# Another hand-written sequence of tasks for a kernel of local attention and an S4 convolution

## The chip, the core and the metric

The kernel runs on one core of a Trainium2 chip. The metric is the device time of one execution, in microseconds. The core has five engines with a queue each, and each queue is worked off in order: TensorE (PE in the profile; its weight loads are shown as PEld), VectorE (DVE), ScalarE (ACT), GpSimd (POOL) and SyncE (SP). In this kernel SP and POOL do little but start transfers (DMA).

## The reference

Two branches see the same input x (2048 positions, 640 channels) and are mixed by a gate.

```
g = sigmoid((x * gate_w).sum(-1))
# A: 32 heads of 20, each position attends to 8 positions, 2 apart, behind it
qkv = x @ wqkv ; logits = q . k[pos - 2*w] * 20**-0.5, w = 0..7 ; a = (softmax(logits) . v) @ wo
# B: a state space filter of 192 states for each channel, as a convolution over 2048 positions
K[d, l] = Re sum_n C[d,n] * exp(dt*A[d,n]*l) * dt*B[d,n]
y = irfft(rfft(pad(x)) * rfft(pad(K)))[:2048] + x * Dskip
return g * a + (1 - g) * y
```

## The kernel before

The work is written as tasks. `Plan.add` puts a task on a list with its possible engines, the tasks it depends on, and the ring of buffers that it takes or gives back. A task issues a few instructions of one engine, or the transfers of one step. Nothing is scheduled at run time: `Plan.order` reads a string of `ORDER` (steps from one task number to the next, with a letter where a task with a choice takes the engine that isn't its first one), and `Plan.emit` issues the tasks in that sequence, each engine keeping its own part of it in order. So the string fixes the order in each of the five queues and, for evictions from PSUM, whether ACT or DVE does them. There are two strings: "main" with 1274 tasks and "tail" with 304.

The names that matter below, in the order in which data flows:

- The front. `turn`, `tev` (L204, L507): PE transposes x in ten pieces, each evicted. `late`, `lev` (L311): 60 pieces of the qkv projection, five matmuls each, in two halves (`late5`, `late5b`), each evicted by `lev`; the first ten are q and k of the first 512 positions. On ACT and DVE the parameters of the filter are made (`SSMParams`: L624 to L661) and stored in ten planes by SP (`sp0` to `sp9`, Sprm). `gate`, `gexp`, `gsig`, `gturn`, `gtwice` (L219 to L239) make the gate.
- The filter generator (`KGen`), ten rounds c = 0 to 9. `L` (L766) loads the planes, `arg` (L801, PE) makes 15 pieces of arguments a round into a ring of two PSUM buffers (`ar`), `act` (L816 Sin, L818 Exp, ACT) evaluates them, `pq` (L838, L840, DVE) multiplies them, three instructions for each of three units, and `kmm` (L856, PE) contracts them: 4 quarters for each unit, of 16 matmuls (32 for the middle unit) in tiles of 128x32 or 64x32. `fin` evicts a round. After rounds 4 and 9 the half of the filter is spread through DRAM (`own`, `other`, `xst`, `xld`: Kx, kc).
- The attention, eight chunks. `prod` (L375, DVE, five a chunk) and `lg` (L381, PE) make logits; `max`, `neg`, `exp`, `sum`, `at` the softmax; `ast` and `asb` take it through DRAM (SP), `vc` loads v (POOL, L368, from vS that `lst` stores); `pv` (L449, DVE) weighs, `gat` (L456, PE) sums, `oT` evicts, `wo` (L480, PE) projects, `ga` evicts with the gate (L489 on ACT, L491 on DVE), `gaS` stores.
- The first transforms: `f1`, `fu`, `fk` (L1300, L1319, PE) of filter and input, with evictions `f1e`, `fue`, `fke` of 1024 columns (halves for some fk). `rows` (L1003, L1004, POOL) loads the input for them in eight steps, each waiting for the one before.
- The tail (`fft_conv`): second transforms `fp` with evictions `sp` in eight blocks, complex products `ta`, `tc`, `Y` on DVE, inverse transforms `inv` with evictions `cp`, then `yp`, evicted and mixed with the attention branch (`tt`, `mx`, `st`), and `out`. SP loads `tphi3` to `tphi7` (PHI, PHX), `paced0` to `paced6` (psi, then gaF).

PE works with different forms of tiles: 128x128 (projections, transforms), 64x128 (arg), 128x32 (logits, kmm), 64x32 (kmm of the middle unit), 128x64 (gat).

## Time and profile before

| | |
|---|---|
| runs | 337.15, 334.77, 336.39 us; median 336.39 |
| span of the profiled execution | 335.4 us (no other time of that execution is shown) |
| first Sin of the generator on ACT | 55.2 us |
| first product of the generator on DVE | 65.5 us |
| end of the main plan, first transform of the tail | 266.5 us |
| last eviction of the output | 328 us |

The page gives busy times of the engines and their share of the span, groups of instructions by source line with the mean duration of one and the idle time ahead of them, and waits by what ended them. A line like L507 or L509 is that of a helper (`evict`), so its groups are told apart by their tiles. A matmul's end is modelled, so what PE waits for is read better from its weight loads (PEld). "issue" is waiting in which no other engine is seen to be the cause.

### The profile page before, as it was taken

Reading aid. Unit: us, or ns where it says so; the run is one execution under the profiler, and the core shown is the slowest. Engines: PE = TensorE matmul, PEld = TensorE weight load, DVE = VectorE, ACT = ScalarE, POOL = GpSimd, SP = SyncE. Lnnn points to the kernel's source line nnn. Section 1 sums busy time; section 2 is a strip of 40 time slices with the busy share of each in tenths; the row PEclk is TensorE's granted clock in tenths of the full one; section 3 lists DMA queues with packets and bytes.
Section 4 is the critical chain, followed back from the end, with each engine's and each line's share of the span. In section 5 each row is a group of like instructions: output and inputs, shape, how many; then the busy total and the mean of one; then the engine's idle time right before and its main releaser. Section 6 shows DMA issues by size and latency. Waiting matters only on the chain. (4 is left out here: it accounts for less than half of the span.)

```text
span 335.4 us, 11982 instructions
## 1 busy us (share of the span) xinstructions
PE 285.5 (85%) x5181; PEld 171.0 (51%) x5214; DVE 294.2 (88%) x401; ACT 293.4 (87%) x433; POOL 62.3 (19%) x94
## 2 busy tenths in 40 slices
PE   0367999997899999999998799999999899996850
PEld 0334563444445555445554344556677676665740
DVE  1997988798989999999999979999686799999881
ACT  1789736999899999999999799999987889998990
POOL 8700043020005000101412341211040000000062
PEclk9999999999999999999999989999999999999985
DMA  8984435437107110524874887365565527666056
GB/s 253 356 264 113 119 91 159 86 91 170 26 9 153 27 24 8 149 62 141 199 190 119 186 208 161 93 118 124 154 207 221 180 64 216 159 123 100 4 136 182
DMA packets 45975, 45.68 MB, mean 136 GB/s; under 512 B 25098, under 2 KB 39738, under 8 KB 45922
## 3 DMA queue, kind: packets, MB, share of 16 engines
q1 hardware_dynamic: 39928, 27.90, 30.3%
q0 software_dynamic: 5248, 16.39, 20.2%
q8 instruction: 41, 0.67, 0.9%
q10 hardware_dynamic: 746, 0.61, 0.6%
q14 instruction: 12, 0.10, 0.1%
HBM read 30.88 MB, written 14.01 MB: 134 GB/s over the span
## 5 line engine op out<-in xcount | busy, mean ns | idle before, releaser
L311 PE MATMUL tb<-bufA 128*128 128x512 bf16 x267 | 73.5, 391 | 4.2 <-issue 1.4
L816 ACT ACTIVATE big<-ar 128x740 bf16<-128x740 int16 (+1 forms) x72 | 56.7, 858 | 1.4 <-PE ar L801 1.2
L818 ACT ACTIVATE big<-ar 128x848 bf16<-128x848 f32 x60 | 50.1, 905 | 0.2
L801 PE MATMUL ar<-Rarg,L 64*128 64x212 bf16 (+4 forms) x600 | 46.5, 253 | 3.5 <-ACT big L816 1.9
L449 DVE TENSOR_TENSOR pv<-vc,asb 128x2048 bf16<-128x2048 bf16 x40 | 48.2, 1217 | 0.3 <-PE tb L456 0.3
L311 PEld LDWEIGHTS <-bufA 128*128 128x128 bf16 x300 | 31.2, 122 | 28.5 <-issue 12.3
L856 PEld LDWEIGHTS <-pt 128*32 128x32 bf16 (+1 forms) x2560 | 25.3, 92 | 35.7 <-issue 33.2
L856 PE MATMUL kps<-qq,pt 128*32 128x21 bf16 (+1 forms) x2560 | 36.6, 173 | 6.0 <-issue 5.1
L838 DVE TENSOR_TENSOR pt<-big 128x1024 bf16<-128x1024 bf16 x48 | 32.8, 701 | 4.3 <-ACT big L816 2.2
L801 PEld LDWEIGHTS <-L 64*128 64x128 bf16 x600 | 20.8, 94 | 25.2 <-issue 22.4
L480 PE MATMUL tb<-wo_sb,oT 128*128 128x320 bf16 x160 | 29.9, 306 | 0.2
L507 ACT ACTIVATE sp_u<-fp 128x640 bf16<-128x640 f32 x31 | 23.9, 953 | 0.8 <-PE fp L1073 0.8
L375 DVE TENSOR_TENSOR prod<-prj 128x2048 bf16<-128x2048 bf16 x20 | 24.0, 1218 | 0.2 <-PE lg L381 0.2
L375 DVE TENSOR_TENSOR prod<-qA,kA 128x2048 bf16<-128x2048 bf16 x20 | 23.9, 1217 | 0.2 <-PE lg L381 0.2
L507 ACT ACTIVATE sp_k<-fp 128x640 bf16<-128x640 f32 x29 | 22.6, 969 | 1.1 <-PE fp L1073 1.1
L456 PE MATMUL tb<-pv,ind 128*64 128x512 bf16 (+1 forms) x192 | 23.2, 353 | 0.0
L368 POOL DMA_DIRECT2D vc<-vS x16 | 11.5, 723 | 59.0 <-DVE pv L449 55.0
L840 DVE TENSOR_TENSOR qq<-big 128x1344 bf16<-128x1344 bf16 x24 | 21.2, 883 | 0.0
L1191 POOL DMA_DIRECT2D out_dram<-ot x14 | 7.7, 558 | 72.3 <-DVE ot L1173 72.3
L1073 PEld LDWEIGHTS <-PHI 128*128 128x128 bf16 x160 | 15.5, 97 | 8.1 <-issue 1.1
L489 ACT ACTIVATE ga<-tb,g_sb 128x320 bf16<-128x320 f32 x29 | 15.6, 550 | 3.4 <-PE tb L480 3.1
L480 PEld LDWEIGHTS <-oT 128*128 128x128 bf16 x160 | 13.1, 98 | 7.1 <-issue 3.1
(171 smaller groups left out, 547.9 us busy)
## 6 DMA issues: line engine op xcount, KB each, us to landing
vc<-vS POOLq DMA_DIRECT2D x16, 327.5 KB, 6.4
xn<-in_A_x_dram SPq DMA_DIRECT2D x4, 640.0 KB
gaS<-ga SPq DMA_DIRECT2D x8, 320.0 KB
Usb<-in_A_x_dram POOLq DMA_DIRECT2D x8, 320.0 KB, 5.7
gaF<-gaS SPq DMA_DIRECT2D x8, 320.0 KB
bufA<-in_A_wqkv_dram SPq DMA_DIRECT2D x3, 800.0 KB
Sprm<-pc SPq DMA_DIRECT2D x10, 240.0 KB
L<-Sprm SPq DMA_DIRECT2D x76, 30.0 KB
```

The costliest lines, as they stand in the source:

```text
L311: nc.tensor.matmul(ppf, self.wq[:, which, kt, e::5], self.xT[:, c0 // 1024, kt, c0 % 1024:c0 % 1024 + SC], start=(kt == 0), stop=(kt == NK ...
L375: nc.vector.tensor_tensor(b[e][:], q[:, e, o:o + C].unsqueeze(1).to_broadcast([128, W, C]), win(k[:, e, :], o, W, DIL, C), ALU.mult)
L449: nc.vector.tensor_tensor(o, vw, b["asb"][:].unsqueeze(2).to_broadcast(sh), ALU.mult)
L456: nc.tensor.matmul(b["op", e][64 * a:64 * a + 64, 0:n, :], ind[:, 32:96], b["pv", e][:, w, a, 0:n, :], start=(w == 0), stop=(w == 3), skip ...
L480: nc.tensor.matmul(apf[:, :320], b["oT"][:, e, i * 128:(i + 1) * 128], wo_sb[:, e, hf * 320:(hf + 1) * 320], start=(e == 0), stop=(e == 4))
L507: nc.scalar.activation(o, i, ACT.Identity)
L801: nc.tensor.matmul(ar[:, g2, a0:a0 + ncol], L[rows, sb, gv, l0:l0 + 128], R[rows, c0:c0 + ncol], start=True, stop=True, tile_position=(64 ...
L816: nc.scalar.activation(d_[:, :, s0 * QW:s1 * QW], ar[:].bitcast(I16)[:, :, 0:2 * (s1 - s0) * QW:2], ACT.Sin, scale=SCL)
L818: nc.scalar.activation(dst[:, gp::2].rearrange("p g s n -> p g (s n)"), ar[:, :, 0:2 * EW], ACT.Exp)
L838: nc.vector.tensor_tensor(pt[:, :, k, :], gg[:, :, ::-1] if k else gg, e1, ALU.mult)
L840: nc.vector.tensor_tensor(qq[:], trg[:, :, KI:].rearrange("p a (v m) -> p a v m", v=2), exq[:, :, KI:].unsqueeze(2).to_broadcast([128, 32, ...
L856: nc.tensor.matmul(kps[32 * g:32 * g + 32, h, NM * ql:NM * ql + NM], pt[rows, k, v, :], qq[rows, k, v, :], start=(g not in started), stop= ...
```

## The change

Only the two strings of `ORDER` change. No task is added or dropped, no instruction differs in form; the sequence does, and for 22 + 22 tasks of "main" and 6 + 7 of "tail" the choice of engine (DVE to ACT, and ACT to DVE).

```diff
 ORDER = {"main": (
-    "7 -7 15 -14 1 1166 -1164 56 -57 3 2 -3 6 1 1 39 -43 1 51A -8A -25 -14 2 38 1D 1 1A -32 33 1A -42 1 69 1 -57 72 -56 57 "
...
+    "7 53 -45 -15 1 3 1 6 -8 -1 4 6 -4 53 -48 -4 1 13 29 1 -29 -10 2 38 1D 1 1 1 1 28 1 1080 -1140 -11 1 4 11D 1 55 -58 1 "
...
 ), "tail": (
-    "3 1A 7 1A -7 1D 1 6 1A -6D 1 1A 10 -5 1A 1 1A 3 13 1D -13 1 1 2 1A 3 1A -3 1A -4 11 1A 6 -11 1A 11 -6 1A 1 1A -41 1 "
...
+    "5 -2 1D 2 5 -4 5D 1 1D 6 -12 1 1 11 13 1 -20 2 -1 2D 20 -2 3 -2 -11 1 -5 1 1 1 3 1 14 -13 2 -1 2 11 -4 1 4 1 1 1 -48 1 "
...
```

Written out by name, the parts of the queues that are spoken of below:

```
DVE, front
- mk5 stt_at near_t1 near_t0 mk7 mk6 tev7 tev5 tev8 lev9 prod00 prod01 gsig lev18 prod02 lev35
+ mk5 lin_t1 stt_t1 stt_at stt_at near_t1 near_t0 mk6 mk7 prod00 prod01 prod02 gsig prod03 lev35
PE, front
- turn7 late3b late8 late8b late6 turn5 late6b turn8 late15 late9 late15b late9b gate late11 late18 late11b late18b
-   lg00 lg01 late35 late25 gturn late35b late25b lg02 late28 late27 arg00000
+ late4 late4b turn6 late9 late9b late7 late7b late1 late1b late15 late15b late11 late11b gate
+   lg00 lg01 late18 late18b late35 late35b gturn lg02 arg00000
PE, a piece of round 3 to 4
- arg40000 kmm222 lg32 lg33 kmm223 arg40001 late40b late43 kmm300 arg40010 arg40100 late43b late45 kmm301 lg34
+ arg30200 late40 late40b arg30201 kmm300 kmm301 kmm302 kmm303 arg30210 lg32 late43 arg40000 arg40001
SP, main
- L0S L1 ast0 L2 asb0 L3 ast1 ... xst1S gaS6 xld1S gaS7
+ L0S L1 ast0 asb0 L2 L3 ast1 ... xst1S gaS6 xld1S gaS7
POOL, main
- consts L0G lst02 vc0 vc256 lst12 wo vc512 dskip lst22 lst32 gst rows0 vc768 rows1 xst0G rows2 vc1024 rows3 rows4
-   xld0G rows5 vc1280 rows6 vc1536 rows7 gates0 vc1792 xst1G xld1G phi0 gates1 phi1 gates2 phi2 gates3
+ consts wo dskip L0G gst lst02 vc0 vc256 lst12 vc512 lst22 vc768 lst32 rows0 rows1 rows2 rows3 xst0G vc1024 xld0G
+   vc1280 rows4 rows5 rows6 rows7 phi0 gates3 gates0 gates1 gates2 phi1 vc1536 vc1792 phi2 xst1G xld1G
SP, tail
- tphi3 tphi4 tphi5 paced0 paced1 tphi6 tphi7 paced2 paced3 paced4 paced5 paced6
+ tphi3 tphi4 tphi5 tphi6 paced0 paced1 paced2 paced3 paced4 tphi7 paced5 paced6
```

On DVE the evictions tev5, tev7, tev8, lev0, lev9, lev14 and lev18 leave for ACT, and mk4, mk8 and lin_t1 come from it. On PE the quarters of kmm, which stood mostly one by one between other tasks, stand in groups of two to six; between neighbouring PE tasks of "main" the form of the tiles changes 380 times in the old sequence and 280 times in the new one.

## The prediction

> **What bounds the kernel now.** The page is read first for whether one engine carries the span, then the busy time by stage, then what each engine waited for.

> ```profile
> span 335.4 us, 11982 instructions
> PE 285.5 (85%) x5181; PEld 171.0 (51%) x5214; DVE 294.2 (88%) x401; ACT 293.4 (87%) x433; POOL 62.3 (19%) x94
> ...
> 65.50:100.00 34.50, 31.05 (x696) 16.11 (x703) 30.55 (x43) 32.24 (x46) 1.93 (x3) 1.00 0.31 72
> 100.00:186.00 86.00, 82.02 (x1885) 43.37 (x1901) 83.50 (x117) 85.85 (x131) 15.68 (x25) 1.00 0.44 108
> 186.00:198.00 12.00, 9.64 (x191) 4.14 (x187) 9.50 (x11) 9.45 (x16) 4.44 (x4) 0.86 0.82 208
> 198.00:235.00 37.00, 35.61 (x989) 20.95 (x986) 36.40 (x46) 36.09 (x53) 8.58 (x13) 1.00 0.59 128
> 235.00:266.50 31.50, 29.41 (x247) 22.31 (x244) 24.81 (x37) 28.09 (x42) 4.37 (x8) 1.00 0.58 197
> ...
> 65.50:266.50 201.00, 187.72 (x3992) 106.88 (x4013) 184.75 (x250) 191.71 (x283) 34.99 (x52) 0.99 0.49 125
> 55.20:266.50 211.30, 197.28 (x4067) 111.15 (x4095) 192.72 (x262) 201.98 (x296) 36.90 (x55) 0.99 0.50 126
> ```

> The columns of a stretch are its length and the busy time of PE, PEld, DVE, ACT and POOL, then the granted clock. No engine carries the span alone. From 55.2 us, where ScalarE's first Sin runs, to 266.5, where the main plan ends, ACT is busy 201.98 of 211.30 (9.3 idle). From 65.5, where the first product of the filter generator runs, DVE is busy 184.75 of 201.00. Its 16.3 us of idle time are 4.0 before 100, 2.5 to 186, 2.5 around 190, 0.6 to 235 and 6.7 at the end. So a new order wins by starting this stretch earlier, by taking work off the two engines in it, or by closing those gaps. What ends the gaps on DVE, and what holds TensorE:

> ```profile
> DVE prj L509 <- PE tb L311: 2.9, 2, 1.7
> DVE big L509 <- PE bp L1300: 2.7, 3, 1.2
> DVE pt L838 <- ACT big L816: 2.2, 1, 2.2
> DVE oT L509 <- PE tb L456: 2.1, 2, 1.8
> ...
> PEld L856 <- issue: 33.2, 108, 2.5
> ...
> 191.39 0.27 PE L856 MATMUL kps<-qq,pt 128*32 128x21 bf16 x15 [2.36 <-issue]
> ...
> 192.00:194.00 2.00, 2.00 (x44) 0.79 (x43) 0.01 (x1) 1.39 (x3) 1.35 (x3) 0.53 0.28 50
> ```

> PE ends three of DVE's four longest groups of waits (2.9+2.7+2.1 = 7.7 us); the fourth, 2.2 us, follows a 2.36 us pause in which PE waited for no engine, after which its clock was 0.53. PE's weight loads stood 33.2 us in 108 waits at L856, where the 128x32 tiles of kmm begin, 0.31 us each.

> **The change, part by part.** Only the sequence and the choice of ACT or DVE for some evictions differ; instructions, transfers and the 18 changes of activation table stay. 22 tasks of the main plan go from DVE to ACT and 22 back.

> *The front.* Now the first Sin waits for PE, and PE for DVE:

> ```profile
> 40.69 3.48 DVE L509 CAST bufA<-ar 128x1024 bf16<-128x1024 f32 x3
> 44.89 0.69 DVE L509 CAST kA<-tb 128x512 bf16<-128x512 f32 x1 [0.72 <-PE tb L311]
> 45.49 2.35 DVE L375 TENSOR_TENSOR prod<-qA,kA 128x2048 bf16<-128x2048 bf16 x2
> 49.67 1.22 DVE L375 TENSOR_TENSOR prod<-qA,kA 128x2048 bf16<-128x2048 bf16 x1
> ...
> 44.09 2.64 POOL L766 DMA_DIRECT2D L<-Sprm  x4 [29.57 <-DMA L<-Sprm]
> 44.69 2.14 PE L219 MATMUL ar<-gw_sb,bufA 128*128 128x1 bf16 x80
> 46.69 2.33 PE L311 MATMUL tb<-bufA 128*128 128x512 bf16 x9
> 52.07 0.40 PE L381 MATMUL lg<-prod,ind 128*32 128x512 bf16 x4
> 53.44 0.52 PE L801 MATMUL ar<-Rarg,L 64*128 64x296 bf16 x8
> 53.88 1.28 ACT L816 ACT_TABLE_LOAD   x1 [2.87 <-PE ar L801]
> 55.18 6.69 ACT L816 ACTIVATE big<-ar 128x888 bf16<-128x888 int16 x9
> ```

> prod02 (49.67 to 50.9) stands behind three big casts, lev9, the gate and lev18; lg02 follows it at 52.07, then a stretch of projections, and only then arg at 53.44. After the change the casts, lev9 and lev18 are on ACT, and prod00 to prod02 run in a row ahead of the gate. They need all ten q and k evictions; the last, lev1, has its projection two pieces ahead of the gate, so at 1.17 us a piece (2.33 for two) it is evicted near 43.2 and prod02 ends near 46.7. The gate's PE work stays where it was, 44.8 to 47.0, as one piece more but the same transposes precede it and PE stalls less on evictions. Then come lg00, lg01, two pieces (2.3), gturn, lg02 and arg near 50.8, with the row's 1.28 us of table load behind gturn's eviction: the first Sin near 52.0, 3.2 us sooner. The ends are 0 (the ten evictions come no sooner) and 6.6 (arg straight behind the gate's PE work, which ends at 46.83, as POOL's issue of L does at 46.73: 53.44 less 46.83). ACT's tasks from the first Sin to the first product are the same, so the first product moves from 65.5 to 62.3.

> *The load of the two engines.* Behind the first Sin ACT has three full transform evictions and two gate evictions fewer, one narrow fewer, two wide oT and kh3 more. DVE, behind the first product, has three transform evictions and two gate evictions more, two wide oT fewer.

> ```profile
> L507 ACT ACTIVATE big<-bp 128x1024 bf16<-128x1024 f32 x15 | 14.9, 1036 | 0.5 <-PE bp L1300 0.4
> L489 ACT ACTIVATE ga<-tb,g_sb 128x320 bf16<-128x320 f32 x29 | 15.6, 550 | 3.4 <-PE tb L480 3.1
> L507 ACT ACTIVATE oT<-tb 128x512 bf16<-128x512 f32 (+1 forms) x19 | 10.0, 565 | 1.0 <-issue 1.0
> L509 DVE CAST big<-bp 128x1024 bf16<-128x1024 f32 x5 | 6.1, 1221 | 2.7 <-PE bp L1300 2.7
> ```

> ACT: -3 x 1.04 - 2 x 0.55 - 0.35 + 2 x 0.57 + 0.4, about -3.0. DVE: +3 x 1.22 + 2 x 0.5 - 2 x 0.6, about +3.5 (on DVE ga and oT are taken as long as on ACT). With idle time unchanged ACT would end at 52.0 + 202.0 - 3.0 + 9.3 = 260.3 and DVE at 62.3 + 184.8 + 3.5 + 16.3 = 266.9. So DVE decides, and everything hangs on its gaps.

> *TensorE's blocks.* kmm, now mostly single quarters between arg and projections, comes in twos to sixes. Changes of tile form between neighbouring PE tasks fall from 380 to 280.

> ```profile
> 208.48 0.17 PEld L856 LDWEIGHTS <-pt 128*32 128x32 bf16 x16 [0.17 <-issue]
> 208.68 0.11 PEld L480 LDWEIGHTS <-oT 128*128 128x128 bf16 x2
> ...
> 210.73 0.27 PEld L856 LDWEIGHTS <-pt 128*32 128x32 bf16 x32 [0.17 <-issue]
> 211.03 0.12 PEld L801 LDWEIGHTS <-L 64*128 64x128 bf16 x4
> ```

> One quarter (x16) holds PE 0.20 us, two in a row (x32) 0.30. So a change removed is worth 0.10 to 0.31 us, a hundred 10 to 31 us of PE; I take 11, as most are kmm's. [...] Either is worth only what DVE or ACT wait for: 83 of the hundred changes go between the first arg of c = 2 and the last of c = 9, and most of that stretch lies between 100 and 235, where DVE had, but for the pause at 190, 2.5 + 0.6 us of gaps. So I take 2.0 of the 4.0 us before 100, 1.2 of the 2.5 around 190 (whether a pause of PE falls on full buffers is chance, half of it), nothing between, and 2.0 of the 6.7 at the end, where DVE's three added evictions fall into its gaps: 5.2 in all, between 0 and 13. DVE then ends at 266.9 - 5.2 = 261.7, ACT by 260.3: the main plan ends 4.8 sooner.

> *Queues.* On SP the attention stores stay in turn, and xld1S stays behind gaS6. On POOL wo and dskip go ahead of L0G into a 29.57 us wait (the row above): nothing, or their issue time if the parameters came earlier. rows0 to rows3 pass vc1024, and rows4 to rows7, the gates and phi1 pass vc1536; pv40 and pv60, which need them, come 10 us or more behind the latest loads by DVE's own work, so nothing, and without that cover up to 6.9 us a row load (the longest of POOL's waits for Usb).

> ```profile
> POOL pace L1003 <- DMA Usb<-in_A_x_dram: 22.5, 5, 6.9
> ...
> 277.00 0.86 SPq L993 DMA_DIRECT2D PHI<-c_phi  x2
> 286.56 14.65 SPq L1092 DMA_DIRECT2D gaF<-gaS  x8
> ...
> L1073 PE MATMUL fp<-big,PHI x80: 296/299/300, 267.2 to 302.7; 128*128 128x320 bf16 x80
> ...
> DMA to landing us min/median/max: 5.7/6.0/7.2
> ```

> *The tail.* One spectrum eviction more goes to DVE (+0.7), but its first comes behind PE's second transform instead of the third (-0.6): 0.1. The PHI load of the last block, the second at 277, now follows gaF's third issue, some 4 us into the row at 286.56, so near 291 on the old clock. Eight blocks of transforms fill 266.6 to 303, 4.5 us each, so its user starts near 298, and a landing of 5.7 to 7.2 us (POOL's PHI loads, the last row) just does: 0 taken, 3 at most.

> **Sum.** 335.4 - 4.8 + 0.1 = 330.7 us of span. The median of the runs, 336.39, lies 1.0 above the profiled span (no other time of that execution is shown), so 331.7.

> **The rivals.** *The gaps stay.* PE is freed where nobody waits for it: the first 4.0 and last 6.7 us stay and the work moved to DVE eats the earlier start: 266.9, 336.9 us with the +0.1. For it: 83 of 100 changes; against: the named PE waits.

> *PE's blocks starve ACT (slower).* ar has two buffers and ACT takes one in 0.74 us (6.69 for nine). Whole blocks of kmm and projections now stand between pairs of arg; every 0.1 us by which one outlasts the pair costs ACT 7.5 us over 75 pairs. From 0.11 us a pair (8.1: the gain and 3.4 us) it is slower than before by 1%; at 0.17, 12.8 us, 344. Against it: the 11 us that PE gains; for it: PE's in-order queue, and that ACT has 9.3 us of idle time to lose from.

> *The clock falls in the new gaps.* PE with less to do pauses longer; the pause of 2.36 us brought 0.53 of the clock and 2.5 us lost on DVE and on ACT (12 less 9.50 and 9.45). Two such more: 336.7. [...]

> **How the numbers follow.** The forecast 0.50, about 324.5 to 333; gaps stay 0.22; starved ACT 0.18; clock 0.06; a mixture 0.04. The low end is nearly all 13 us of DVE's gaps closed (331.7 less 7 of the 7.8 left). The high end takes in the gaps and a starvation of 0.1 us a pair (331.7 + 7.5), leaving about 2 in 10 out: 324.5 to 339. One per cent, about what a measurement here can tell from no change, is 3.4 us. Faster by over 1% (below 333.0): 0.53; within: 0.28; slower: 0.19.

> **What would show it.** Front: first Sin near 52, products of L838 from 62. Load: ACT's busy time behind its first Sin near 199, DVE's behind its first product near 188. Blocks: PEld's waits at L856 in number halved. Gaps: DVE idle near 11 us from the first product to the main plan's end. Wrong if the first Sin stays at 55, if DVE's idle time stays at 16 or more, or if ACT's waits on ar at L801 exceed 8 us.

## The result and the profile after

The changed kernel takes 332.88 us (median of 4 runs, 331.15 to 336.2) beside 336.77 for the kernel before on the same chip: a ratio of 0.9868 [0.982, 0.9917]. A second set of runs of the same kernel, below called the repeat, gave 332.6 and 0.9844 [0.9802, 0.9887]. The forecast was 331.7, between 324.5 and 339.0. The medians are over all runs of a kernel, while every ratio leaves out the runs in a slower state with a lower clock (one here, one each of the repeat, old_fours and new_shift8 below, and six of front_shift's twelve, whose other six have a median of 339.3). The profile taken with the first set shows a stretch of half clock right behind the gate (48.27 to 51.68 us), and its first Sin at 54.2, so the profile of the repeat (334.15 us, span 332.4) is read here. Source lines of the changed kernel are 6 lower than before; in the kernels below they differ by a few lines too.

The busy time by stage, repeat; the columns are those of the prediction's first fence:

```profile
62.40:100.00 37.60, 35.18 (x844) 18.98 (x850) 35.08 (x46) 35.19 (x51) 2.28 (x3) 1.00 0.30 70
100.00:180.00 80.00, 76.79 (x1819) 41.86 (x1833) 78.79 (x111) 79.59 (x123) 10.25 (x15) 1.00 0.44 111
180.00:218.00 38.00, 32.85 (x778) 17.26 (x776) 33.97 (x42) 35.01 (x53) 13.29 (x18) 0.91 0.75 179
218.00:235.00 17.00, 14.47 (x356) 11.10 (x357) 16.81 (x29) 15.95 (x23) 1.98 (x3) 1.00 0.33 73
235.00:262.30 27.30, 25.86 (x206) 19.42 (x206) 23.21 (x27) 23.36 (x34) 1.19 (x2) 1.00 0.39 131
62.40:262.30 199.90, 185.16 (x3997) 108.61 (x4018) 187.86 (x251) 189.11 (x280) 28.98 (x41) 0.98 0.46 116
51.00:262.30 211.30, 196.19 (x4084) 113.83 (x4106) 197.03 (x266) 200.07 (x293) 31.98 (x46) 0.98 0.47 118
```

The first Sin runs at 51.0 us instead of 55.2, the first product at 62.4 instead of 65.5, and the main plan ends at 262.0 instead of 266.6 (tail's first transform; the stretches above run to 262.3, those of before to 266.5). DVE's busy time behind the first product is 187.86 (184.75 before) and its idle time 199.90 less 187.86, 12.0 us (16.3 before). By stage the idle time is 2.5, 1.2, 4.0, 0.2 and 4.1 us: the stretch before 100 us and the end became tighter, and as much as at the end is now lost from 180 to 218, where the granted clock is 0.91.

The front of the repeat, instructions in order of time on DVE, PE and ACT (start, length, what ended an idle time in brackets):

```profile
41.21 1.22 DVE L369 TENSOR_TENSOR prod<-qA,kA 128x2048 bf16<-128x2048 bf16 x1
42.64 1.23 DVE L369 TENSOR_TENSOR prod<-qA,kA 128x2048 bf16<-128x2048 bf16 x1 [0.21 <-ACT qA L501]
46.49 1.23 DVE L369 TENSOR_TENSOR prod<-qA,kA 128x2048 bf16<-128x2048 bf16 x1 [2.62 <-PE lg L375]
...
43.97 2.14 PE L213 MATMUL ar<-gw_sb,bufA 128*128 128x1 bf16 x80
46.04 0.61 PE L375 MATMUL lg<-prod,ind 128*32 128x512 bf16 x8
46.59 2.35 PE L305 MATMUL tb<-bufA 128*128 128x512 bf16 x9
48.87 0.22 PE L229 MATMUL ar<-ident,ob 128*16 128x128 bf16 x1
49.24 0.54 PE L795 MATMUL ar<-Rarg,L 64*128 64x296 bf16 x8
...
50.98 2.27 ACT L810 ACTIVATE big<-ar 128x888 bf16<-128x888 int16 x3
```

Waits of the repeat (total, times, longest): PE's weight loads over the whole run, then DVE from the first product to the end of the main plan:

```profile
PEld L795 <- issue: 32.8, 90, 0.6
PEld L305 <- issue: 10.9, 50, 0.6
PEld L850 <- issue: 8.5, 34, 1.7
...
DVE prod L369 <- PE lg L375: 2.7, 2, 2.1
...
DVE big L503 <- PE bp L1294: 0.8, 2, 0.4
...
DVE oT L503 <- PE tb L450: 0.7, 2, 0.5
```

Weight loads of kmm wait 34 times for 8.5 us instead of 108 times for 33.2; those of arg wait 32.8 us instead of 22.4. DVE's three groups that the prediction named (prj, big, oT, 7.7 us in this stretch) are down to 0.8 + 0.7 = 1.5, as prj no longer waits for PE there, and prod behind lg, 0.4 before, has 2.7.

### The profile page after: what moved, and what is told of

The parts are those of the page before. It is cut to its first block, busy times and chain, and to the rows that moved or that the text cites. A ratio compares the mean times of both kernels' runs of the same rounds, so it can differ in the third digit from the quotient of the medians.

```text
span 334.4 us, 11969 instructions
## 1 busy us (share of the span) xinstructions
PE 288.4 (86%) x5214; PEld 174.6 (52%) x5214; DVE 295.6 (88%) x402; ACT 293.0 (88%) x432; POOL 62.7 (19%) x94
## 4 chain that ended last, share of the span: by engine, by line
PE 50%; ACT 28%; DVE 13%; issue 4%; DMA 2%; POOL 0%; POOLq 0%; ACTq 0%
PE tb L305 16%; PE ar L795 8%; PE tb L474 5%; PE kps L850 4%; ACT big L812 4%; ACT bufA L501 4%; PE bp L1294 4%; ACT big L810 4%; PE tb L450 3%; PE fp L1067 3%; ACT tt L1164 3%; DVE tc L1095 2%; PE lg L375 2%; DVE bufA L503 2%; ACT bufA L810 2%
## 5 line engine op out<-in xcount | busy, mean ns | idle before, releaser
L305 PE MATMUL tb<-bufA 128*128 128x512 bf16 x300 | 79.4, 400 | 0.6 <-ACT qA L501 0.4
L795 PE MATMUL ar<-Rarg,L 64*128 64x212 bf16 (+4 forms) x600 | 47.8, 254 | 4.2 <-ACT big L810 1.5
L305 PEld LDWEIGHTS <-bufA 128*128 128x128 bf16 x300 | 32.2, 122 | 31.0 <-issue 13.5
L474 PE MATMUL tb<-wo_sb,oT 128*128 128x320 bf16 x160 | 28.1, 309 | 1.5 <-ACT ga L483 1.4
L850 PEld LDWEIGHTS <-pt 128*32 128x32 bf16 (+1 forms) x2560 | 23.2, 92 | 10.2 <-issue 8.3
L850 PE MATMUL kps<-qq,pt 128*32 128x21 bf16 (+1 forms) x2560 | 27.0, 175 | 1.5 <-issue 1.4
L501 ACT ACTIVATE sp_k<-fp 128x640 bf16<-128x640 f32 x31 | 21.0, 804 | 2.6 <-PE fp L1067 2.2
L450 PE MATMUL tb<-pv,ind 128*64 128x512 bf16 (+1 forms) x192 | 22.1, 354 | 0.7 <-ACT ga L483 0.6
L474 PEld LDWEIGHTS <-oT 128*128 128x128 bf16 x160 | 14.9, 100 | 9.1 <-issue 3.7
L501 ACT ACTIVATE sp_u<-fp 128x640 bf16<-128x640 f32 x28 | 19.1, 805 | 0.3 <-PE fp L1067 0.3
```

The source lines that it names most:

```text
L305: nc.tensor.matmul(ppf, self.wq[:, which, kt, e::5], self.xT[:, c0 // 1024, kt, c0 % 1024:c0 % 1024 + SC], start=(kt == 0), stop=(kt == NK ...
L450: nc.tensor.matmul(b["op", e][64 * a:64 * a + 64, 0:n, :], ind[:, 32:96], b["pv", e][:, w, a, 0:n, :], start=(w == 0), stop=(w == 3), skip ...
L474: nc.tensor.matmul(apf[:, :320], b["oT"][:, e, i * 128:(i + 1) * 128], wo_sb[:, e, hf * 320:(hf + 1) * 320], start=(e == 0), stop=(e == 4))
L501: nc.scalar.activation(o, i, ACT.Identity)
L795: nc.tensor.matmul(ar[:, g2, a0:a0 + ncol], L[rows, sb, gv, l0:l0 + 128], R[rows, c0:c0 + ncol], start=True, stop=True, tile_position=(64 ...
L850: nc.tensor.matmul(kps[32 * g:32 * g + 32, h, NM * ql:NM * ql + NM], pt[rows, k, v, :], qq[rows, k, v, :], start=(g not in started), stop= ...
```

## Experiments

Each median stands beside that of the kernel before in the same set. That was 337.35 in the first four, 337.98 in the next four and 337.04 in the last four.

### The change by parts: repeat, main plan, tail, front

Edits, all in the strings of ORDER: the repeat is the changed kernel as it is; main_only has the new main and the old tail; tail_only the old main and the new tail; front_only has the new sequence up to the first Sin (act00000), then the old one, and the old tail.

> The changed kernel once more, for a second profile and a tighter ratio. The prediction's theory: 0.985 to 0.99 of before. Theory of the clock: the runs spread over some 5 us between them, and each run's time follows its mean granted clock (0.983 at 331 us, 0.965 at 336 us), because the sequence leaves pauses that now and then halve TensorE's clock for 3.4 us.

> The new main sequence with the old tail sequence. Prediction's theory (the main plan ends 4 to 5 us sooner, the tail changes by 0.1): as the full change, 332 to 333 us, within 1 us of it. Rival (part of the gain is lost again in the tail, by one more eviction on DVE and the PHI load moved behind gaF): 1 to 2 us faster than the full change.

> The old main sequence with the new tail sequence. Prediction's theory: the same as before within 0.7 us. Rival (the late PHI load holds the last block): 1 to 3 us slower than before.

> The new sequence up to the first Sin of the filter generator, then all remaining tasks in the old sequence, old tail. Prediction's theory (the front is worth 3.2 us, and what follows keeps its own gaps): 2 to 3 us faster than before, 333.5 to 334.5. Rival, after the profile of the changed kernel (first Sin at 54.2 and not 52.0): within 1 us of before.

| kernel | median, us | ratio to before |
|---|---|---|
| repeat | 332.6 | 0.9844 [0.9802, 0.9887] |
| main_only | 331.94 | 0.9839 [0.9791, 0.9887] |
| tail_only | 337.5 | 0.9992 [0.9962, 1.0022] |
| front_only | 334.43 | 0.9924 [0.9894, 0.9955] |

The tail is worth nothing that can be told. By the ratios front_only is 0.0076 of 337.35 faster, 2.6 us, and what stands behind the front in the main plan adds 0.0085, 2.9 us. In front_only the first Sin comes 3.8 us sooner (55.2 to 51.4), but the first product only 0.8 (65.5 to 64.7), and the pause of 1.9 us that PE makes at 82.4 in the kernel before is gone. So how much of the 2.6 us is the earlier start is not shown; the sections on pauses come back to it.

### Blocks of kmm alone, and the new sequence without them

old_fours: in the old sequence the four quarters of a unit stand where the first one stood. new_spread: in the new sequence each kmm waits its turn until two other PE tasks have gone.

```diff
 old_fours, PE
- arg40000 kmm222 lg32 lg33 kmm223 arg40001 late40b late43 kmm300 arg40010 arg40100 late43b late45 kmm301 lg34
+ arg40000 lg32 lg33 arg40001 late40b late43 kmm300 kmm301 kmm302 kmm303 arg40010 arg40100 late43b late45 lg34
 new_spread, PE
- arg30201 kmm300 kmm301 kmm302 kmm303 arg30210 lg32 late43 arg40000 arg40001
+ arg30201 kmm300 arg30210 lg32 kmm301 late43 arg40000 kmm302 arg40001 late43b kmm303
```

> The old sequence with one thing changed: the four quarters of kmm of each unit stand together (where the first one stood), so that changes of tile form between neighbouring PE tasks fall from 380 to 276, as in the new sequence (280). Everything else keeps its old turn. Theory A (the blocks alone are worth little, because in the old sequence DVE and ACT hardly wait for PE between 100 and 235): PEld's waits at the kmm line fall from 108 to about 35, but the time falls by less than 1 us, 336.5 to 337.4 beside the 337.35 of before on this chip. Theory B (the freed time of TensorE is what the body gained): 2 to 4 us less, 333.4 to 335.4. Theory C (blocks ahead of arg starve ACT): slower, over 338.5, with ACT's waits on ar doubled.

> The new sequence with its blocks undone: the quarters of kmm are put back one at a time between other PE tasks, two tasks apart, so that changes of tile form rise from 280 to 361. Beside the changed kernel's 332.6. Theory A (blocks hardly matter): 332 to 333.6, and ACT's waits on ar stay. Theory B (blocks are the body's gain): 334.5 to 336, since the body gained about 2.7 us beyond the front. Rival (blocks delay arg and cost ACT): faster, below 331.5.

old_fours took 347.04, 1.0289 [1.0243, 1.0336], further than theory C asked for, and new_spread 351.86, 1.0408 [1.035, 1.0466], outside all three of its theories. Waits of old_fours, then of new_spread:

```profile
PE kps L852 <- issue: 6.7, 5, 2.0
...
DVE prj L505 <- PE tb L307: 7.1, 6, 2.6
DVE prod L371 <- PE lg L377: 6.6, 5, 3.5
ACT ga L485 <- PE tb L476: 4.8, 5, 1.7
ACT big L812 <- PE ar L797: 4.6, 7, 1.8
```

```profile
ACT E L503 <- PE kps L852: 8.2, 3, 3.9
ACT big L812 <- PE ar L797: 6.7, 9, 2.4
...
DVE pt L834 <- PE kps L852: 4.7, 2, 2.9
```

In old_fours everything that stood between the quarters comes later, and DVE and ACT wait for it, as theory C had it. Its weight loads of kmm wait 14.1 us instead of 33.2, but those of arg, the projections, lg, gat and wo wait more, so that the six lines together rise from 78.1 us to 84.6. There are also five pauses in the middle of kmm that no engine causes (kps <- issue, 6.7 us). new_spread doesn't answer the question: put off by two tasks at a time, kmm came so late that the buffers of products (pt <- kps) and the eviction of a round (E <- kps) waited for it. It removed the blocks and made kmm late as well.

### Pauses without a cause: where they stand

The pauses of PE in the main plan that no engine ends, of about half a microsecond and more, stand at fixed numbers of its instructions. Counted by weight loads (a matmul here comes with a weight load, 5181 beside 5214 in the profile of before, so it counts as two instructions), before pauses at instructions 1466, 6074 and 6842, old_fours at 1978, 5050, 6074, 6586 and 6842, and the changed kernel at 7356. All are 186 or 188 more than a multiple of 256. (Two more, at the tail's first transform and at yp, keep their place in the work when the numbers shift, and are not meant here.) The instruction queue q8 moves packets of 16 KB (16,384 bytes each in the two profiles of the main comparison), 41 of them in the kernel before and 40 in the changed one. Only PE has about 10,400 instructions (5181 and 5214 beside 401 of DVE, 433 of ACT and 94 of POOL), so I take the queue for PE's, and one packet then holds some 256: an estimate, 10,395 by 41. The next kernel moves these borders: main_only with 64 more copies of the one five-column matmul at the very start, which write the same values again.

```diff
+        for _ in range(65):
             nc.tensor.matmul(lt[:, 0, 0:5], g5[:], at_.ident[0:5, 0:5], start=True, stop=True)
```

> New main sequence, old tail (331.94, the base), with 64 more copies of the one five-column matmul at the very start of PE's program: 128 PE instructions more. PE's pauses without a releaser near 189 (before) and 207.5 (after) begin while a 16 KB packet of the instruction queue is on its way. If PE's program is fetched in blocks of about 256 instructions, the pause moves by half a block: to about 205.5 or 209 at the earliest places that hold the same instructions, and another, now between two blocks, can grow or go. Theory A (pauses are fetches and their place is chance): the pause of 1.1 to 1.7 us near 207.5 is no longer between the same two quarters of kmm, and the time is within 1.5 us of 331.9, either way. Theory B (the pause belongs to the work there, not to the fetch): same place in the sequence, same length, and the time differs only by what the 64 matmuls cost the front (0 to 2 us).

It took 343.18, 1.0172 [1.0129, 1.0214], 11 us over its base. The front didn't move (first Sin 51.3 beside 51.4), and the main plan ended at 271.2 beside 261.4. So it isn't the copies' own time. Its waits, its timeline around the longest pause, and the stages around it (PE, PEld, DVE, ACT, POOL, clock, DMA share):

```profile
PE kps L851 <- issue: 7.9, 5, 2.5
```

```profile
144.73 0.39 PE L851 MATMUL kps<-qq,pt 128*32 128x21 bf16 x33
147.62 0.37 PE L851 MATMUL kps<-qq,pt 128*32 128x21 bf16 x31 [2.51 <-issue]
```

```profile
142.00:144.00 2.00, 1.94 (x146) 1.71 (x146) 2.00 (x4) 1.98 (x3) 0.00 (x0) 1.00 0.98 233
144.00:146.00 2.00, 1.12 (x41) 0.54 (x38) 1.97 (x4) 1.99 (x4) 0.00 (x0) 1.00 0.44 79
146.00:148.00 2.00, 0.38 (x32) 0.34 (x32) 2.00 (x2) 0.25 (x1) 0.00 (x0) 1.00 0.19 33
```

The pauses are in new places (1212, 2492, 4540, 6844, 7612 and 8122, again 186 or 188 over a multiple of 256), and there are six of them instead of one. Ahead of this one the DMA engines are 0.98 busy. Theory A fits what a pause is, and was wrong on its size: "within 1.5 us" was 11. Theory B, that the pause belongs to the work, fell.

### The clock

fill puts eight matmuls, overwritten by the next one, in front of a gather of the fifth chunk (the second of its three groups; the expectation miscounts it as the third), ahead of PE's 0.85 us wait for the softmax, in main_only.

```diff
+                    for a in (0, 1) * (4 if c0 == 1024 and e == 2 and w0 == 0 else 0):
+                        nc.tensor.matmul(b["op", e][64 * a:64 * a + 64, 0:n, :], ind[:, 32:96], b["pv", e][:, 0, a, 0:n, :], start=True, ...)
                     for w in range(w0, w1):
```

> New main sequence, old tail (331.94, the base), with eight more matmuls of PE in front of one gather (third gather group of the fifth chunk, near 194.9): they write what the next matmul writes anew, and stand where PE then waits 0.85 us for the softmax. Every 3.41 us window at half clock seen so far comes directly behind a window of the same length in which PE was busy 0.64 or less; the window ahead of 199.4 has 0.60. With the filler it has about 0.8. Theory A (the clock is granted by how busy PE was in the window before): the half-clock window at 199.4 is gone, and the time is about 1.4 us lower, near 330.5. Theory B (the windows come from something else, such as the pause of the fetch or the power of the other engines): it stays, and the time is 331.9 to 332.6, the filler costing up to 0.7.

331.45, 0.9835 [0.979, 0.9879]. The half clock at 199.4 is gone in its profile, and one at 215.3 is there. Beside main_only (0.9839) no difference can be told. The filler also moved the borders behind it by 16 instructions, and the pause at 207.5 is gone too, so this run alone doesn't show what the filler does. Nor is the missing half clock a sign for theory A: new_shift8 below, which has no filler, has none near 199.4 either, and one at 214.8. And "every" in the expectation doesn't hold: ahead of the half clock at 48.27 in the first set PE is busy in all of the 3.41 us.

### The same borders in the old sequence

old_shift is the kernel before with 40 more copies (80 PE instructions), front_shift is front_only with 40, fours_shift old_fours with 36, and new_shift8 main_only with 4 (8 instructions); the edit is that of fetch128 with another count.

> The kernel before with 40 more copies of the one five-column matmul at the start of PE's program: 80 PE instructions more, so that the borders of its fetch blocks (every 256 instructions, seen as pauses at instruction numbers of 186 to 188 over a multiple of 256 in every kernel so far) fall elsewhere in an unchanged old sequence. Before pauses 2.0 us at 82.3, 2.45 at 188.9 and 0.74 at 207.3 at such borders, and loses one half-clock window behind the second. Counted from its trace, at this place every block of 256 instructions takes more than 3.7 us. Theory A (the new sequence's gain behind the front, about 2.7 us, is that its borders fall better): no pause over 0.5 us, and 333 to 335.5 beside the 337.4 to 338.0 of before. Theory B (the order itself made the gain; the place of the borders hardly matters to the old one): 336.5 to 338.5.

> Control of the shift: new main sequence, old tail (331.94, the base), with 4 more copies of the five-column matmul, 8 PE instructions. Counted from the trace of the base, borders 8 instructions later cross the same work (only the block that ends at 207.5 takes under 3.7 us). Theory A (fetch128 lost its 9 us by the place of the borders): 331 to 333. Theory B (extra matmuls at the start themselves upset the program, by whatever way): slower by 2 us or more.

> old_fours (kmm in fours in the old sequence, 347.04) with 36 more copies, 72 PE instructions. old_fours paused 0.93 at 92.6, 1.53 at 166.7, 2.0 at 194.5, 2.13 at 205.1 and 1.25 at 212.7 at borders of fetch blocks, 7.8 us in all, and had three half-clock windows from 208.8. Counted from its trace, at this place only two blocks take less than 3.7 us, none under 3.2. Theory A (the blocks of kmm cost by outrunning the fetch): most pauses go, and the time falls by 6 us or more, to 341 or below. Theory B (grouping itself delays what DVE and ACT wait for): 344 to 348.

> front_only (the new front, then the old sequence, 334.43) with 40 more copies, 80 PE instructions, as in old_shift. Front_only pauses 1.44 us at 186.0 and 0.5 at 203.4 at borders, and has half-clock windows behind the first and at 301. If theory A of old_shift holds, the front's gain and the borders' gain add up: 330.5 to 332.5, as fast as the changed kernel without any change behind the front, or faster. Under theory B: 333.5 to 335.5.

| kernel | median, us | ratio to before | ratio of its base |
|---|---|---|---|
| old_shift | 339.97 | 1.0091 [1.0058, 1.0125] | 1 |
| new_shift8 | 331.28 | 0.9833 [0.9794, 0.9872] | 0.9839 |
| fours_shift | 343.87 | 1.0211 [1.0169, 1.0253] | 1.0289 |
| front_shift | 342.25 | 1.0067 [1.0025, 1.0108] | 0.9924 |

The control stayed: 8 instructions more cost nothing, and the pause at 207.5 shrank to 0.17 us. But the old sequence became slower, not faster: the way in which I had chosen the place, by how long each block of 256 instructions takes, seems to have missed what holds a fetch up. Timeline rows of old_shift, front_shift and fours_shift:

```profile
185.87 0.33 PE L857 MATMUL kps<-qq,pt 64*32 64x21 bf16 x26
189.58 0.23 PE L857 MATMUL kps<-qq,pt 64*32 64x21 bf16 x6 [3.37 <-issue]
```

```profile
188.19 0.23 PE L854 MATMUL kps<-qq,pt 64*32 64x21 bf16 x6 [3.69 <-issue]
```

```profile
193.33 0.69 PE L476 MATMUL tb<-wo_sb,oT 128*128 128x320 bf16 x2 [3.50 <-issue]
```

All three stand at instruction 6074, where the kernel before has its pause of 2.36 us. In fours_shift the instructions there are projections in full tiles, so neither kmm nor a change of tile form makes the pause. What may make it is seen in the DMA queues of the kernel before, first from 184 to 188.5 us, then from 188.5 to 190 (packets, MB, share of the 16 engines):

```profile
q0 software_dynamic: 174, 0.58, 68.1%
q1 hardware_dynamic: 347, 0.22, 29.4%
```

```profile
q1 hardware_dynamic: 464, 0.25, 96.3%
q8 instruction: 1, 0.02, 6.1%
```

From 182 to 188 loads of v, of the input's rows and of the planes L fill the engines, 97.5% in the first answer, and no packet of the instruction queue moves. The packet of q8 starts at 188.54, takes 1.46, and PE goes on at 191.39. In old_shift the same transfers come 1 to 2 us sooner, the packet starts at 186.47, and PE, which came to the border at 186.2 instead of 189.0, goes on at 189.58. Stages of old_shift:

```profile
183.00:185.00 2.00, 1.85 (x79) 1.09 (x78) 2.00 (x4) 2.00 (x5) 0.00 (x0) 1.00 1.03 208
185.00:187.00 2.00, 1.21 (x35) 0.65 (x32) 1.74 (x2) 1.64 (x3) 0.00 (x0) 1.00 1.06 186
187.00:189.00 2.00, 0.00 (x0) 0.00 (x0) 0.00 (x0) 0.00 (x0) 0.00 (x0) 0.89 0.82 160
```

For two microseconds PE, DVE, ACT and POOL do nothing. That the pause is PE waiting for its own instructions, held up behind data, is carried by the fixed instruction number, by the place of the packets, and by the full DMA engines: of the 28 such pauses of the 14 profiles 26 have a DMA share of 0.9 or more over two of the four microseconds before them, where 37% of all moments of the stretch would. The exceptions are 69.6 in fetch128 and 93 in old_fours, where PE ran through the 256 instructions ahead in 1.6 and 2.2 us. No transfer was taken away to test it from the other side. The trace doesn't tell when a fetch was asked for, but over the 14 profiles the next packet starts 0.9 us (median) after PE passes a border where the DMA share is under 0.6, and 2.1 us after it where the share is 0.9 or more; ahead of the pause at 189 in the kernel before it was 4.1 us.

Theory A of old_shift, front_shift and fours_shift fell as it was put. fours_shift came down by 0.8% but not to 341. At nearly the same borders (72 and 80 instructions) it stands 343.87 less 339.97, 3.9 us, behind old_shift. In the two profiles the pauses at borders add up to 4.9 and 4.3 us, so most of the 3.9 seems to be what grouping kmm itself costs in the old sequence. front_shift lost 0.0143 of 337 us, 4.8, against front_only, and the main plan in its profile ends 4.2 us later. Against old_shift, with the same shift, it is only 0.0024 (0.8 us) faster, and the intervals overlap: with its borders moved, the front's gain of 2.6 us can't be told from none.

## Why the prediction was right, and where it wasn't

**Front: right in its times, with one step off.** First Sin at 51.0 (forecast 52.0), first product at 62.4 (62.3). The step "prod00 to prod02 run in a row ahead of the gate" failed: prod has two buffers, its first is given back by lg00, lg00 stands behind the gate on PE, and so prod02 waited 2.62 us and ended at 47.7, not 46.7. It cost nothing, since arg waits for what comes before it on PE: the gate, lg00, lg01, two pieces of projections, gturn and lg02, until 49.24. That queue was 1.6 us faster than forecast: the gate ran from 43.97 to 46.1, not to 47.0, and the pieces behind it to 48.9.

**Load: right.** ACT behind its first Sin is busy 200.07 us (199.0), DVE behind its first product 187.86 (188.3).

**TensorE's blocks: the step that failed.** The prediction took the fewer changes of tile form as the reason for closing the gaps. PE's weight loads do wait less: the issue waits of the six lines that had most (kmm, arg, projections, lg, gat, wo) fell from 78.1 to 65.0 us, 13 beside the 11 forecast. PE's busy time in the stretch fell by only 2.6 us (187.72 to 185.16). The 0.31 us that the prediction took for a wait at kmm at most is a mean that takes in the pauses of 2.0 and 2.5 us. But old_fours makes the same cut in changes of form (380 to 276), its waits of the six lines rise to 84.6 us, and it loses 3.9 us or more. So fewer changes do not by themselves free PE or close a gap; whether they helped inside the new sequence isn't shown, as new_spread doesn't answer it. What one change of form costs, 0.10 to 0.31 us in the prediction, was my estimate from the rows of weight loads; no run shows it apart from the place of the work, and in old_fours, with 104 changes fewer, the time rose from 337.35 to 347.04 us.

**Gaps: 4.3 us closed, 5.2 forecast, not where forecast.** Before 100 they closed by 1.5 (2.0 forecast), at the end by 2.6 (2.0). From 100 to 235 they stayed: 5.6 before, 5.4 after, where 1.2 was to go. The pause around 188 is gone, but a pause at a border of 1.65 us at 207.4 and two half-clock windows came in its place. So the term for the gaps stood at nearly its size, but not for the reason and not in the places that the forecast gave: that the total came out within 1 us or so is partly luck. main_only leads front_only by 5.5 us when the eighth round's products start (179.2 beside 184.7), is 0.9 behind at the tenth's (214.8 beside 213.9), and 1.1 ahead at the tail.

**Tail and sum.** 0.1 was forecast and 0.9992 [0.9962, 1.0022] measured. The main plan ended 4.6 us sooner (262.0 instead of 266.6) where 4.8 was forecast. The 1.0 between span and time was 1.75 (334.15 less 332.4). By the same difference the profiled run of before, 335.4, is that of 337.15, and not one near the median as the sum had it; this cancels in the forecast, which is the median less 4.7. The low end, 331.7 less 7, is 324.7 and not 324.5.

**The rivals.** *Gaps stay* (336.9): no, DVE's idle time fell from 16.3 to 12.0. *Starved ACT*: no, behind the first Sin its waits for arg come to 2.7 us, the longest 1.6; in old_fours, with 8.1 us of them, it did happen. *Clock in new gaps*: partly, inside the gain. The repeat's stages:

```profile
195.40:198.80 3.40, 2.03 (x44) 1.28 (x40) 3.00 (x6) 3.39 (x6) 2.16 (x2) 1.00 0.50 114
198.90:202.20 3.30, 3.30 (x20) 1.26 (x17) 3.30 (x6) 2.29 (x4) 0.30 (x1) 0.50 0.83 153
205.70:209.10 3.40, 1.63 (x130) 1.23 (x130) 3.40 (x4) 2.52 (x4) 2.15 (x4) 1.00 0.51 144
209.20:212.40 3.20, 3.20 (x103) 1.57 (x90) 1.91 (x2) 2.42 (x3) 3.02 (x6) 0.50 0.96 193
```

Two windows at half clock (0.50), each behind a window in which PE was busy 60% and 48%. The longest idle time in the first is 0.85 us, so it isn't one long pause that counts. The kernel before had one such window in this stretch.

What stays open is how much of the gain, in the front and behind it, belongs to the order as such. An estimate from the traces: from the first product to the tail the kernel before takes 201.1 us with 4.9 us of pauses at borders, main_only 198.6 with 1.1, new_shift8 197.0 with none. Without the pauses that leaves 196.2, 197.5 and 197.0; the five profiles with the old order behind the front, kmm not grouped, lie between 196.0 and 198.7, the six with the new one between 197.0 and 198.9. So behind the first product the new order shows no gain other than fewer pauses. The estimate counts each pause as lost in full, which no run shows. Nor was it tried apart what the choice of engines, the turn of the loads on POOL and SP, and the place of kmm do behind the front. Moving the borders by 128 instructions cost the new sequence 11 us, and moving them by 80 cost the old one 2.9, as much as or more than the gain in question. At its own borders the new sequence is good, at 8 further as well. new_shift8 (331.28) and fill (331.45) lie below main_only, but not by more than can be told from it.

## What to carry to other kernels

When TensorE pauses and no engine is the cause, look for the packets of its instruction queue and what data fills the DMA engines ahead of them; here such pauses took 0.5 to 3.7 us, and the longest stood behind bursts of loads of several hundred kilobytes (0.80 MB from 184 to 188.5 us in the kernel before), mostly in runs of small matmuls. Before crediting an order of work with one per cent, shift the whole program by some harmless instructions and measure again, since the place of the borders alone was worth up to three per cent here (fetch128 1.0172, main_only 0.9839). And grouping matmuls of one form cost more than it gave in the old sequence (old_fours 1.0289), where others waited for what stood between them.
